# A tuned attention and MLP kernel: the second head of unit 9 is turned too, and the written-out order of the main loop is made anew

## The chip, the cores and the metric

The kernel runs on one core of a Trainium2 chip. A core has the engines TensorE (PE; its weight loads are shown as PEld), VectorE (DVE), ScalarE (ACT), GpSimd (POOL) and SyncE (SP, which here only issues DMAs). Each runs its own instructions in order and waits on semaphores for the others. The metric is the time of one execution on the device, in microseconds (us).

## The reference

One transformer block on 2048 tokens of 448 features. `xn` is the layernorm of `x`; the result is `x`, plus attention of `xn` with 16 query heads of 28 and one shared key and value head, plus an MLP (layernorm, 448 to 1792, GELU, 1792 to 448) of `xn`.

```python
q = (xn @ wq)            # 16 heads of 28
k, v = xn @ wk, xn @ wv  # one head, shared by all
scores = einsum("bhqd,bkd->bhqk", q, k) * 28 ** -0.5
p = softmax(scores, axis=-1)
attention = einsum("bhqk,bkd->bhqd", p, v) @ wo
y = layernorm(xn)
mlp = gelu(y @ w1 + b1) @ w2 + b2
out = x + attention + mlp
```

## The kernel before

The queries are cut into 4 blocks of 512, the heads into 4 groups of 4. A block and a group make a *unit*: 16 units, each with 4 heads of 512 queries against 2048 keys, the keys in 16 *key tiles* of 128. The kernel first normalises and projects, then runs the MLP, and beside the MLP it begins the attention; what is left of attention is the main loop.

There are two ways to the exponentials of a head.

- *Not turned.* A first pass computes the scores with queries on the partitions (TensorE, L668, 16 matmuls of 128x512) only to reduce each to its maximum (VectorE, L669). The maxima go into two spare rows of the query operand, and a second pass computes the scores with keys on the partitions, the maximum already taken off (TensorE, L1104, 16 matmuls); ScalarE exponentiates them from the PSUM bank into a tile `p` (L1105).
- *Turned.* One pass computes the scores with queries on the partitions (TensorE, L704, 16 matmuls). VectorE moves each to the SBUF tile `raw` with its maximum (L705); four such make a tile of 128 queries by 2048 keys. ScalarE exponentiates that in two halves (L722), four DMAs of 256 KB store it to DRAM in `td` (L725), and later it is loaded by quarters of the keys (`quarter`, L913, two DMAs of 512 KB a quarter), where VectorE turns blocks of 32x32 into `p` (L1080, one instruction for two key tiles).

Which heads are turned is in `TURNED`, pairs of unit and head: head 3 of every unit, and head 2 of units 11, 13 and 15, 19 in all. The tile `raw` has two buffers (`RAWS = 2`), so the first L705 of a tile waits for the store of the tile two before it.

From the `p` tiles of all four heads the value product goes, key tile by key tile, into one bank `po` (L1068; L1051 for the last unit, which is done in two halves): four matmuls with 32 columns of weights each, side by side in the array. A run of such products is called a *burst* here. Then the sums are divided out (`norm_jobs`) and multiplied by `wo` (`o_jobs`, L944 to L946).

The main loop goes over 128 steps of two key tiles, taken in 64 pairs, four pairs a unit. What an engine does in which order is nothing but the order in which the program issues it, and that is written out: `ORDERS` has a string for each pair, and each letter issues something. `s` is a score matmul of L1104 with its exponential, `m` a maximum (L668 and L669), `t` a step of a turned head (L704 and L705), `x` half an exponentiation of `raw` (L722, with the stores behind the second half), `T` a turn (L1080), a digit so many key tiles of the value product, as far as their `p` tiles are issued, `e` the maxima of the next unit, `n` a step of the division, `o` a step of the product with `wo`, and `|` the second step of the pair, with its loads. `BANKS` gives for each matmul that takes a PSUM bank in the loop which of the seven it takes. Beside the MLP, 192 turned steps and 390 maxima are done at a fixed pace that no table sets; the strings hold the rest, 112 `t`, 330 `m`, 720 `s` and 152 `T`. The loads of quarters are issued four steps ahead by SyncE, those of queries by GpSimd.

Of the kernel before, what the change touches and what calls it, by code (L numbers as in the profile page):

```python
# [26 lines left out]
SCALE = DH ** -0.5  # L27
PAIRS = 13
ORDERS = (
    "|sssmsmssmtmssmmmTssTtss",  # L30
    "sm|ssss3smsttsmsstTssT",
    "smmss|sm3essmtsTxmsssstsT",
    "T|x4mmsstTssmsssssm2smss",
    "mmsssmTxxsstmTmss4smn|sntsss",
    "smm2nmsmsmmsststst|Tntxsmss3enmTsmnxs",
    "ssssm3TsmnsmssttmsTsss|n",
    "ssxnmsTtsnxn22msnsmmmssssnsTs|",
    "ssstT2smsst|msmssssTs",
    "ssT|2msntmsTstsxmmnsmmx4smsnnstmsts",
    "|ssmTnmnnTsses3smssstssmsmxmm",  # L40
    "sns3sssTsmm|smnnstmmtm2snssmmsntT",
    "sssTssxnssm4mnsnmmsss|mtsT",
    "sss|2mmsmssxtmnnTsmssnxs3snsT",
    "|tmsmsssstsnssTTe21tmssssx",
    "sT|smsss1nn4Tmmxsntnssmmsmsss",
    "sssTmsnnms3Tmsmsmtnsssms|sto",
    "ntsT4xxsnsnTms|stmnstsmmssmnsnsns",
    "o2nooTmsmosmosesnsmttmTsm3msmssmsmsno|mnxos",
    "smTssTmx|4stsmnstsmsstsss",
    "Ts|mmssT3tsmmmsmsmxmtsossmsnmsnmtsmm",  # L50
    "sns|sTsssnx6nmssmsmTmtsossm",
    "smsnssmssmmstosmst|sexxTTnss",
    "ssTmsn213|snsmsmtnsnsTosmmssntns",
    "sstTsmxstxsts31mstssmTtnss|s",
    "Tsss2msnsnstsmmm|sTssssmxxn3",
    "tennmTTstnsssnmssnss4sms|sms",
    "mssmsssn|tssmTmsTsn3nttssmms",
    "ssxxmmTnsmssst1T3mntsm|ssnsss",
    "Ttsnsxtn21s|mnsssxTsmmses2msmss",
    "ssmtssmsnsstnT|s4xTmsmssms",  # L60
    "nssnstsxmTsm2mTsssssnsmtt|2s",
    "Tssnmnmtsnstsxxtmmss3on|mmosstnnsTsms",
    "smT|osso4smesnsmsmmmsssnmsnTs",
    "smnst2x2T|tsmsnsmssmosmxmosTssns",
    "msn3|sTmsmnsmossmnsnttsmsstxsTxmos",
    "sTs5mstsmsstsTmmmsso|tssttmsx",
    "sTtsoxssststnmnms2xsmmssxnsmnT|s",
    "ssmsnns5smnesTstmssm|osmssT",
    "sstsnss|Tmsnn3smtssmmnTsss",
    "ms|stnxsTm4Tsmssnssssss",  # L70
    "mm|xT2mtnmssnsm11mnnstssmsstsssTs",
    "sTm2|esnnsmssmtssmnnxmsmxsntT3msstmms",
    "so|tTstssmmTmm1n3smnssmsssnmmnsms",
    "|sTsTm5nTmnmnsmsnntssTss",
    "Ts|ssTTTss5msesnmsm",
    "ssssxssT111s|TTTs",
    "snmsssss|nTxsTT5Tntsn",
    "smmsmsssmsnttsssnnTm|mxsm3mmmnosTs",
    "Tmsmms|smsn4nmtxesnmstsnTsssmomsts",
    "nmn3|osmsmsmsmosmnmsossTmTssomsmsn",  # L80
    "4on1TnnmssmnTtsssssm|1smsmssms",
    "sTm3oTmmssnTnsmnm|omssssT",
    "msmxnsnomTssTtt4nstnmm|TssnTs",
    "ssm|sneonTnTssmsmm4TmssT",
    "mTmsmnsns5xmsTTTs|mmsss",
    "stsT4mmxnsss|snnossnmssTss",
    "sxnssmm31ssmTsssssm2Tmsnm|s",
    "ssmsmTs1enssnssss|snTs",
    "ss4ssssssTsnns|2Tss",
    "TnssssssTssT1n|11T",  # L90
    "nnTsss|ssTTsT3ss",
    "ssssssTn5n|sToTTs",
    "sTssosTs|sossoT212T",
)
BANKS = (
    "0163240513642015346203412503125064312560314526045231604521306451230465123460531246053214062153046123"
    "5024361502431652034150632451603124560312453610245631024563214056325140632510436251043652014630521463"
    "0524136052130465213406253140625310462531046253014652301426531024635102463152046312054631024563012456"
    "3102451630245610324605312460531240653214605231460521346503241560324150632145306214350621436502143650"
    "2416350241630524165340231654023165420635412063541205634120563421603542160345216034521603542160534216"  # L100
    "5034215603241653204165320145603124560314620346205134620513642105436120534610523460154236014523604152"
    "3604123560412536014256302145630214562340165234012635401623405612340561234051624305162430521463052164"
    "3052164350126431502643152064312654031265401326504150326451034265013425610234560124351602435160352416"
    "0352416035421630541263540126345012603145263015426301546230154623015642301546320154620314520631425603"
    "1426503142650312456031245601324651032465103426510342650143256013425610342615361304256013246051362540"
    "1362541063421503416025341625304162530416253041625301462503146520314650321460531240653241524063152631"
    "564023156402315640263415026341250631420563124056312405631240563124053124053124053124053124031"
)
# [10 lines left out]
def block_kernel(ctx, tc, x, wq, wk, wv, wo, w1, b1, w2, b2, out):  # L119
# [16 lines left out]
    def heads_of(u):  # L136
        return 4 - sum(v == u for v, _ in TURNED)

# [438 lines left out]
    for c in range(NCH):  # L577
        if c + 1 < NCH:
            center, turn = norm_parts(c + 1, False, bank=lambda shape: (qbank, mtile)[next(turns) % 2](shape))
        for i in range(4):  # L580
# [24 lines left out]
            if i in ((1, 3), (1, 2), (1, 3), (0, 2))[c]:  # L605
# [90 lines left out]
    def turned_scores(i):  # L696
        for t in range(CT):
# [4 lines left out]
            for n in range(4):  # L702
# [4 lines left out]
                                  op0=ALU.mult, op1=ALU.max, accum_out=m3[:, n:n + 1])  # L707
                if (t, n) == (0, 3) and 0 < i < len(TURNED) - 1:
                    load_m(*TURNED[i + 1], q3[1 - i % 2])
                if n == 3:  # L710
                    dve.tensor_reduce(m3[:, 4:5], m3[:, 0:4], axis=AX.X, op=ALU.max, negate=True)  # L711
                    exps.extend((TURNED[i], t, raw, m3, h) for h in range(2))
                yield
# [492 lines left out]
```

## Time and profile before

| | |
|---|---|
| median of 3 runs | 1054.6 us (1054.35 to 1054.74) |
| the profiled execution | 1055.69 us, span 1052.8 us |
| TensorE busy | 1043.8 us, 99% of the span |
| VectorE busy | 926.9 us, 88% |
| ScalarE busy | 720.6 us, 68% |
| GpSimd busy | 563.1 us, 53% |
| DMA | 226.17 MB, 215 GB/s on average |

An engine's busy time is the union of its instructions. Matmuls overlap: the next one starts before the last has ended, so what a matmul costs is read from the distance of starts, in the timeline. In a row of the timeline stand the start, the length, the engine, the line of the program, the operation, what it writes and reads, and in brackets how long the engine was idle before it and what ended that. In a row of the groups stand the count, the busy time, the mean length in ns, and the idle time before. The main loop begins at about 481 us and takes the rest of the span; the score matmuls of unit 8 begin at 767.3 us, of unit 12 at 907.0 and of unit 14 at 978.4.

### The profile page before, as it was taken

Reading aid. Unit: us, or ns where it says so; the run is one execution under the profiler, and the core shown is the slowest. Engines: PE = TensorE matmul, PEld = TensorE weight load, DVE = VectorE, ACT = ScalarE, POOL = GpSimd, SP = SyncE. Lnnn points to the kernel's source line nnn. Section 1 sums busy time; section 2 is a strip of 40 time slices with the busy share of each in tenths; the row PEclk is TensorE's granted clock in tenths of the full one; section 3 lists DMA queues with packets and bytes.
Section 4 is the critical chain, followed back from the end, with each engine's and each line's share of the span. In section 5 each row is a group of like instructions: output and inputs, shape, how many; then the busy total and the mean of one; then the engine's idle time right before and its main releaser. Section 6 shows DMA issues by size and latency. Waiting matters only on the chain.

```text
span 1052.8 us, 17905 instructions
## 1 busy us (share of the span) xinstructions
PE 1043.8 (99%) x5773; PEld 708.9 (67%) x5773; DVE 926.9 (88%) x1962; ACT 720.6 (68%) x1224; POOL 563.1 (53%) x704
## 2 busy tenths in 40 slices
PE   9999999999999999999999999999999999999998
PEld 8778888888888888886455545655456555456545
DVE  7889999999999899999798889788788789999775
ACT  6775555656565665556898888688878785865692
POOL 6678787677766777865145353153334233434130
PEclk9999999999999999999999999999999999999999
DMA  8865455667776767984879688687889879898791
GB/s 274 250 217 164 116 148 150 172 166 192 190 184 170 203 183 181 276 215 138 243 205 247 204 232 257 204 237 222 249 253 255 243 237 280 271 279 261 236 354 38
DMA packets 224593, 226.17 MB, mean 215 GB/s; under 512 B 18622, under 2 KB 190804, under 8 KB 224500
## 3 DMA queue, kind: packets, MB, share of 16 engines
q1 hardware_dynamic: 212084, 204.06, 67.0%
q0 software_dynamic: 11008, 20.40, 7.3%
q8 instruction: 45, 0.74, 0.3%
q10 hardware_dynamic: 1408, 0.57, 0.2%
q14 instruction: 48, 0.39, 0.1%
HBM read 129.24 MB, written 94.49 MB: 213 GB/s over the span
## 4 chain that ended last, share of the span: by engine, by line
PE 94%; DVE 3%; DMA 1%; ACT 1%; SPq 0%; issue 0%; ACTq 0%; DVEq 0%
PE po L1068 20%; PE m L1104 16%; PE m L668 16%; PE m L787 12%; PE ph L262 11%; PE m L704 7%; PE qp L262 3%; DVE mx L669 1%; PE ph L265 1%; PE ph L267 1%; PE m L944 1%; PE m L946 1%; PE m L945 1%; DMA td<-raw 1%; PE po L1051 1%; PE m L1051 1%
## 5 line engine op out<-in xcount | busy, mean ns | idle before, releaser
L669 DVE TENSOR_REDUCE mx<-m 128x1 f32<-128x512 f32 x720 | 463.6, 683 | 54.6 <-PE m L668 51.9
L1105 ACT ACTIVATE p<-m 128x512 f32<-128x512 f32 x622 | 323.6, 623 | 90.1 <-PE m L1104 88.8
L668 PE MATMUL m<-ks,qm 128*128 128x512 f32 x720 | 277.7, 401 | 1.1 <-DVE mx L669 0.6
L1104 PE MATMUL m<-xh,ks 128*128 128x512 f32 x720 | 229.8, 405 | 2.1 <-DVE raw L705 1.1
L1068 PE MATMUL po<-p,vs 128*32 128x512 f32 x1664 | 221.8, 596 | 0.0
L705 DVE TENSOR_SCALAR_CACHE_REDUCE raw<-m 128x512 f32<-128x512 f32 x304 | 202.4, 686 | 20.0 <-PE m L704 12.5
L1104 PEld LDWEIGHTS m<-xh,ks 128*128 128x128 f32 x720 | 131.6, 188 | 69.2 <-ACT p L1105 16.6
L722 ACT ACTIVATE raw<-raw,m 128x1024 f32<-128x1024 f32 x152 | 170.3, 1158 | 3.2 <-DVE m L711 3.1
L668 PEld LDWEIGHTS m<-ks,qm 128*128 128x128 f32 x720 | 134.2, 188 | 55.9 <-issue 12.6
L1080 DVE STREAM_TRANSPOSE p<-quarter 128x1024 f32<-128x1024 f32 x128 | 155.5, 1229 | 4.9 <-PE m L1104 3.1
L752 ACT ACTIVATE hx<-ph,b1t 128x512 f32<-128x512 f32 x55 | 37.9, 688 | 150.5 <-PE ph L267 99.0
L1068 PEld LDWEIGHTS po<-p,vs 128*32 128x32 f32 x1664 | 54.7, 109 | 105.0 <-issue 101.4
L704 PE MATMUL m<-ks,q 128*128 128x512 f32 x304 | 119.0, 398 | 0.0
L768 POOL TENSOR_TENSOR hl<-hx,hh 128x512 fp32r<-128x512 f32 x56 | 72.7, 1298 | 32.4 <-ACT hh L766 32.3
L787 PE MATMUL m<-w2h,hl 128*128 128x448 f32 x224 | 81.3, 367 | 0.0
L787 PE MATMUL m<-w2h,hh 128*128 128x448 f32 x224 | 81.3, 366 | 0.0
L787 PE MATMUL m<-w2l,hh 128*128 128x448 f32 x224 | 81.2, 366 | 0.0
L756 POOL TENSOR_TENSOR hz<-hz,hx 128x512 f32<-128x512 f32 x56 | 72.8, 1300 | 4.6
L761 POOL TENSOR_TENSOR hx<-hx,hz 128x512 f32<-128x512 f32 x56 | 72.6, 1297 | 4.7
L704 PEld LDWEIGHTS m<-ks,q 128*128 128x128 f32 x304 | 57.0, 188 | 20.2 <-issue 2.5
L1068 PE MATMUL po<-xh,vs 128*32 128x512 f32 x256 | 68.7, 596 | 0.0
L633 POOL DMA_DIRECT2D xh<-qd x60 | 38.0, 634 | 56.7 <-PE m L1104 34.4
(198 smaller groups left out, 1527.8 us busy)
## 6 DMA issues: line engine op xcount, KB each, us to landing
td<-raw SPq DMA_DIRECT2D x304, 256.0 KB
quarter<-td SPq DMA_DIRECT2D x146, 512.0 KB
xh<-qd POOLq DMA_DIRECT2D x48, 168.0 KB, 5.6
qd<-qe SPq DMA_DIRECT2D x24, 256.0 KB
a<-in_A_x_dram SPq DMA_DIRECT2D x24, 224.0 KB
qm<-qd SPq DMA_DIRECT2D x96, 56.0 KB
qm<-qd POOLq DMA_DIRECT2D x84, 56.0 KB, 4.9
ad<-a SPq DMA_DIRECT2D x16, 224.0 KB
```

The costliest lines, as they stand in the source:

```text
L262: pe.matmul(ps, w, v, start=(n == 0), stop=False)
L668: pe.matmul(pm, qm[:, t * P:(t + 1) * P], ks[:, n * CW:(n + 1) * CW], start=True, stop=True)
L669: dve.tensor_reduce(mx[:, CT * j + t, n:n + 1], pm, axis=AX.X, op=ALU.max)
L704: pe.matmul(sc, q3[i % 2][:, t * P:(t + 1) * P], ks[:, n * CW:(n + 1) * CW], start=True, stop=True)
L705: dve.tensor_scalar(raw[:, n].rearrange("p r (b i) -> p b r i", i=32), sc.rearrange("p (b r i) -> p b r i", r=4, i=32), SCALE, -3e38, op0= ...
L722: act.activation(raw[:, rs], raw[:, rs], AF.Exp, bias=m3[:, 4:5], scale=1.0)
L756: pool.tensor_mul(hz, hz, hx)
L787: pe.matmul(m2[k], h[:, k * P:(k + 1) * P], w[:, ft, :], start=(ft == 0 and i == 0), stop=(ft == NF - 1 and i == 2))
L1068: pe.matmul(po[32 * j:32 * j + 32, :], vs[:, kt, :], ps.pop((u, kt, j)), start=(kt == 0), stop=(kt == NT - 1))
L1080: dve.transpose(p.rearrange("p k (g j) -> p g k j", j=32), part[:, :, 32 * k:32 * k + 64].rearrange("p g (k j) -> p g k j", j=32))
L1104: pe.matmul(s, ks[:, kt * P:(kt + 1) * P], qss[u][:, j, :], start=True, stop=True)
L1105: act.activation(p, s, AF.Exp, scale=SCALE)
```

## The change

Head 2 of unit 9 is turned as well, 20 heads in all. All 64 strings and the table of banks are new. The strings hold 128 `t`, 314 `m`, 704 `s`, 160 `T`, 64 `x` (56 before) and 72 digits (95 before); the digits add up to 254 in both, and of the 256 key tiles 5 are left for after the last string (3 before). Of the tables the diff shows the pairs that the text speaks of.

```diff
 ORDERS = (
 ...
-    "smTssTmx|4stsmnstsmsstsss",
-    "Ts|mmssT3tsmmmsmsmxmtsossmsnmsnmtsmm",
+    "sxsm4xTtsnsmm|sssttstsnsxnxsTs",
+    "tsnsTs6Ttmsststsossmssso|",
 ...
-    "ssxxmmTnsmssst1T3mntsm|ssnsss",
-    "Ttsnsxtn21s|mnsssxTsmmses2msmss",
+    "T|sxsmottnsssmmsmsmxtm3T1msmmtsnnsss",
+    "Tn|smnssse2smssmsmsnTsss",
 ...
-    "sTs5mstsmsstsTmmmsso|tssttmsx",
-    "sTtsoxssststnmnms2xsmmssxnsmnT|s",
-    "ssmsnns5smnesTstmssm|osmssT",
-    "sstsnss|Tmsnn3smtssmmnTsss",
+    "ssT5sTTmtsmTnsnmss|s",
+    "o|TTs4snsnmmsmnmTsTssmnsmx",
+    "T|Tsnsss4essmstTsmTmo",
+    "ssntsTsmx4TnnmTsT|sss",
 ...
-TURNED = tuple((u, j) for u in range(16) for j in ((3, 2) if u in (11, 13, 15) else (3,)))
+TURNED = tuple((u, j) for u in range(16) for j in ((3, 2) if u in (9, 11, 13, 15) else (3,)))
```

On TensorE, in unit 10 before, two bursts of two key tiles stand seven matmuls apart (L1068; a key tile is four products, whose `p` tiles lie in buffers named `p` and `xh`):

```order
L668 MATMUL m_9680<-ks,qm_162 128x512
L1068 MATMUL po<-p,vs 32x512 x8
L668 MATMUL m_9702<-ks,qm_162 128x512
L704 MATMUL m_9707<-ks,q_165 128x512
L668 MATMUL m_9712<-ks,qm_162 128x512
L1104 MATMUL m_9715<-xh,ks 128x512
L1104 MATMUL m_9718<-xh,ks 128x512
L1104 MATMUL m_9722<-xh,ks 128x512
L668 MATMUL m_9725<-ks,qm_163 128x512
L1068 MATMUL po<-p,vs 32x512 x5
L1068 MATMUL po<-xh,vs 32x512 x2
L1068 MATMUL po<-p,vs 32x512
```

About the same number of scores into the loop, the new order has:

```order
L1104 MATMUL m_9813<-xh,ks 128x512
L668 MATMUL m_9817<-ks,qm_164 128x512
L668 MATMUL m_9820<-ks,qm_164 128x512
L1068 MATMUL po<-p,vs 32x512 x18
L1068 MATMUL po<-xh,vs 32x512
L1068 MATMUL po<-p,vs 32x512
L668 MATMUL m_9848<-ks,qm_164 128x512
L668 MATMUL m_9851<-ks,qm_164 128x512
L1104 MATMUL m_9854<-xh,ks 128x512
```

The two bursts of two are one of five. Over the loop 76 bursts have become 69.

On VectorE, the tile of turned scores that is begun soonest after the exponentiation of the tile two before it. Tiles are counted through the loop from 0. Before, it is tile 16, in the second of the pairs `ssxxmm...` and `Ttsnsx...` above; the last row is its first eviction, and the rows begin behind the second `x` of tile 14 and one reduction:

```order
L669 TENSOR_REDUCE mx<-m_8388 128x1
L1080 STREAM_TRANSPOSE p<-quarter 128x16x2x32
L669 TENSOR_REDUCE mx<-m_8399 128x1
L705 TENSOR_SCALAR raw,m_8347<-m_8411 128x4x4x32
L1080 STREAM_TRANSPOSE p<-quarter 128x16x2x32
L669 TENSOR_REDUCE mx<-m_8433 128x1
L705 TENSOR_SCALAR raw,m_8347<-m_8438 128x4x4x32
L711 TENSOR_REDUCE m_8347<-m_8347 128x1
L669 TENSOR_REDUCE mx<-m_8445 128x1
L912 MEMSET quarter 1x1 x2
L1080 STREAM_TRANSPOSE p<-quarter 128x16x2x32
L705 TENSOR_SCALAR raw,m_8473<-m_8474 128x4x4x32
```

In the new order it is tile 11, which begins with `tsnsTs6...`; the second `x` of tile 9 is the one behind the 4 of the pair ahead of it, and is issued just ahead of the first row:

```order
L1080 STREAM_TRANSPOSE p<-quarter 128x16x2x32
L705 TENSOR_SCALAR raw,m_7440<-m_7441 128x4x4x32
L669 TENSOR_REDUCE mx<-m_7450 128x1
L669 TENSOR_REDUCE mx<-m_7453 128x1
L912 MEMSET quarter 1x1
L705 TENSOR_SCALAR raw,m_7440<-m_7467 128x4x4x32
L705 TENSOR_SCALAR raw,m_7440<-m_7470 128x4x4x32
L705 TENSOR_SCALAR raw,m_7440<-m_7476 128x4x4x32
L711 TENSOR_REDUCE m_7440<-m_7440 128x1
L1080 STREAM_TRANSPOSE xh<-quarter 128x16x2x32
L912 MEMSET quarter 1x1
L705 TENSOR_SCALAR raw,m_7505<-m_7506 128x4x4x32
```

All four evictions of tile 10 now stand between, and fewer reductions; the first eviction comes behind nine instructions instead of eleven, the memsets left out.

More of the change, by code (lines that the diff above doesn't have):

```diff
@@ L29 @@
 ORDERS = (
[L30 to L48, printed above, removed]
-    "smTssTmx|4stsmnstsmsstsss",
-    "Ts|mmssT3tsmmmsmsmxmtsossmsnmsnmtsmm",
[L51 to L56, printed above, removed]
@@ L70 @@
[L70 to L83, printed above, removed]
@@ L84 @@
[L84 to L93, printed above, removed]
+    "ssmsmssmmmssmTmssTs|ss",
+    "tss|4TtstssmsstmsmstsssT",
+    "Tsxsm|4estssmsmssmtsmsmTss",
+    "ssxssTTms5smsmssmmmsms|s",
+    "sstssxmTtxm3mmnmsnstTssns|ssms",
+    "Tss3|stnnmssmmssmtssTsxss",
@@ new lines @@
+    "smT|nssxs6Teststmsmsstssnsnn",
+    "TsnssT|mss3tsmsnstsmmsssmmx",
+    "sTxsmsnns|s4Tmsmtsssmsnss",
+    "nssnT|tsT3sstsstsmmsntsssx",
+    "Tst|smsx4nnnTesmsmnsmtssssxss",
+    "ssm4Tsmmssmss|nnstsmTsss",
+    "|snTnsnm2ssmmsmssmsssmsmttxT3msm",
+    "sstnTs|nssmmsmxT3smsmsnnntsssmm",
+    "tmmsxsns|s3TstmesmtsTnssxsnss",
+    "n|Tts5nxsmsssmTstmsnmsss1nss",
+    "|nmstmtssTmstTsssms4omsmmomsssn",
+    "sss|onnmTsmmxn3sTmemnsotssstosss",
+    "mmxnT|tss3smsnmnsmmssmssmsTsnmms",
+    "sxsm4xTtsnsmm|sssttstsnsxnxsTs",
@@ new lines @@
+    "tsnsTs6Ttmsststsossmssso|",
+    "nTs2s|mssmmntsssstttssssm3To",
+    "3xnxTsmss|nmsnmTmsnemsssxomsssmsm",
+    "|sTssnsnsTsmontsnmmnmtxssts4smsm",
+    "|ssmntTsnssTxstmxstm4mtsnsnstsms",
+    "sns|xTs5nxesmnmstsssnstmsssT",
+    "T|snsnomstsmssstsTttss2sns",
+    "|ssmmssmmtxnnm5xTmstssmssnTsss",
+    "T|sxsmottnsssmmsmsmxtm3T1msmmtsnnsss",
+    "Tn|smnssse2smssmsmsnTsss",
+    "sstnx|mx4nTtsmstsssnmmmsssTsns",
+    "TssT3|stssnmmssssxsnss",
+    "m|mx3Tstsstsnmmmmmssnm4oooooTmtssnonsmsosmsm",
@@ new lines @@
+    "sTn|tmmxT4xsmsmsmssmntsmststnnsss",
+    "|smtsmTsm3stemsssmmmsTnmsmsmnss",
+    "xTmmn4|ssmssnmmsnnsmtTsssntxsss",
+    "ssT5sTTmtsmTnsnmss|s",
+    "o|TTs4snsnmmsmnmTsTssmnsmx",
+    "T|Tsnsss4essmstTsmTmo",
+    "ssntsTsmx4TnnmTsT|sss",
+    "sssnmnnmt4tnsstsxmsm|mTnmxossssmnsT",
+    "ns|Toesssnmmststnsnmmntxxtmmm4mmssmmsmsmsT",
+    "|ssTssmnnssmmT5mmsstsnstsms",
+    "T|mssmtmomsstTsm2sntsmmssstmsxs",
+    "T|mnmmT5msmnTTsstnsssss",
+    "Tn4sTmssnm|TnsmsnTsss",
+    "TTsxs4men|sssnsssTT",
@@ new lines @@
+    "sTsnTssTx51snTm|msmss",
+    "mmssmsxnmssTssmnn2mnmsmsTstssn|",
+    "ss1ssm|tsmnssmttTttsxoxmt4esoosnnmssmmT",
+    "ssonssmtT|sn3smmnssmssmnnmTss",
+    "xossxTsmomTt5mos|msnmssmnmsmssss",
+    "|sTmTsnTs3msntostsnToss",
+    "smsmmnsTTtsnsTsn6|Tss",
+    "TstmsnmtnTostsxmsTe7Txnmssm|ts",
+    "Tnnssmnosmsmn|TmxxnttTsTosss",
+    "s|TTst6tsmmmsnnssmxmsss2sss",
+    "TmtststTssts3xnnxmmsssmsmnnmsxsm|s",
+    "ssTs3ensnsTssns|ssss",
+    "sT3s|nssssTssssn3sns",
+    "Ts|snssssT2nnTssT",
+    "TsTsTss2ssnn|Tss",
@@ L94 @@
+    "ssss2TsTsooso4TsoT|",
+    "sssTssssT|s3TT",
 )
 BANKS = (
[L96 to L105, printed above, removed]
@@ L106 @@
-    "1362541063421503416025341625304162530416253041625301462503146520314650321460531240653241524063152631"
-    "564023156402315640263415026341250631420563124056312405631240563124053124053124053124053124031"
+    "0163240516324053126543126043512604352106342510634251063425016324051632450163245013465201345620135640"
+    "2135640213546023150426314502631450236451203645102364150236145023641502346510324653102465301425603145"
+    "2063145206345120163452061345260314526031456230145632104562314056234105623401526354021635410256431025"
@@ new lines @@
+    "6431026540635142063510462504635120641325063412506342105634251064235106425316042530416523041562031465"
+    "2103465210346521304652130465132064532104653210463045621340526314052631450264352106435210463521046352"
+    "1064532106453126045132604513624015362453016243501264350126435012645031642501346250143560214365021436"
+    "5021436510423651402635401263540126345012506342156043201456320146503421650342165304261354601235406213"
+    "5402615324103416520431650234160523416052431605431260541302564325160425361402610523460512346051234061"
@@ L108 @@
+    "5342016532401635204165302416530246153206543120643512046351024631052460351420653210465231046532106532"
+    "4106532406513245061324506132405163025461302564130526134052164350216043521604351260435612045361240356"
+    "1203456102435604132560143520641352601453601245631024651302465132046513204635104635210462315046231506"
+    "42351604325610345216304521630452163045216304521630452130452130452130415230415"
 )
-TURNED = tuple((u, j) for u in range(16) for j in ((3, 2) if u in (11, 13, 15) else (3,)))
+TURNED = tuple((u, j) for u in range(16) for j in ((3, 2) if u in (9, 11, 13, 15) else (3,)))
```

7 lines of the change are left out of this document (removed).

## The prediction, made before the change was run

> **What bounds the kernel now.** I read the page's busy times first, then the windows of the main loop, then the waits of TensorE, and only then single instructions.
>
> ```profile
> span 1052.8 us, 17905 instructions
> PE 1043.8 (99%) x5773; PEld 708.9 (67%) x5773; DVE 926.9 (88%) x1962; ACT 720.6 (68%) x1224; POOL 563.1 (53%) x704
> 480.00:1020.00 540.00, 537.75 (x3252) 288.04 (x3254) 458.86 (x939) 424.35 (x791) 202.30 (x323) 1.00 0.82 244
> 767.30:978.40 211.10, 211.10 (x1287) 115.52 (x1286) 188.61 (x381) 154.05 (x287) 81.84 (x129) 1.00 0.86 260
> 907.00:978.40 71.40, 71.40 (x433) 39.86 (x433) 67.45 (x133) 45.51 (x87) 29.44 (x45) 1.00 0.86 261
> PE m L1104 <- DVE raw L705: 1.1, 1, 1.1
> PE m L668 <- DVE mx L669: 0.6, 1, 0.6
> DVE mx L669 <- PE m L668: 51.9, 51, 4.2
> ```
>
> The window rows give the length, the busy time of PE, PEld, DVE, ACT and POOL, the granted clock, the DMA share and GB/s. From 480 to 1020 us, which is the main loop, TensorE is busy 537.75 of 540 us at full clock. VectorE is the runner-up, 188.61 of 211.1 us in units 8 to 13 and 67.45 of 71.4 us in the last two of them. TensorE waits for VectorE a microsecond at a time, VectorE for TensorE 51.9 us in all. So the time of the loop is the sum of what TensorE issues. But a busy TensorE is not one at its peak, so the price of a matmul has to come from the distance between starts:
>
> ```profile
> 700.51 0.41 PE L1104 MATMUL m<-xh,ks 128*128 128x512 f32 x1
> 700.85 1.92 PE L1068 MATMUL po<-p,vs 128*32 128x512 f32 x16
> 703.47 0.59 PE L1068 MATMUL po<-xh,vs 128*32 128x512 f32 x1
> 703.90 0.59 PE L1068 MATMUL po<-xh,vs 128*32 128x512 f32 x1
> 704.42 0.50 PE L668 MATMUL m<-ks,qm 128*128 128x512 f32 x1
> 704.76 0.40 PE L1104 MATMUL m<-xh,ks 128*128 128x512 f32 x1
> 705.00 0.40 PE L704 MATMUL m<-ks,q 128*128 128x512 f32 x1
> 705.24 0.63 PE L1104 MATMUL m<-xh,ks 128*128 128x512 f32 x2
> 705.71 0.39 PE L668 MATMUL m<-ks,qm 128*128 128x512 f32 x1
> 705.93 0.39 PE L704 MATMUL m<-ks,q 128*128 128x512 f32 x1
> 706.16 1.58 PE L1104 MATMUL m<-xh,ks 128*128 128x512 f32 x6
> 700.92 3.57 PE po L1068 x32
> 707.75 1.85 PE po L1068 x16
> ```
>
> The first number of a row is the start. From 704.76 to 706.16 six matmuls start, 0.235 us each, though one lasts 0.40. The last two rows are from the chain that ended last: a burst of four key tiles holds 3.57 us, one of two 1.85, so a key tile of the value product costs 0.86.
>
> **The change part by part.**
>
> *Matmuls.* A head that is turned has no pass for maxima (16 matmuls of L668) and no scores at L1104 (16), but 16 at L704. On TensorE 16 go: 16 x 0.235 = **-3.8 us**. They all stand in the main loop, since the stage ahead of it still takes 192 turned and 390 maximum steps. The two ends of this term are 0.235, the plain distance, and 0.40, the busy time (6.4 us); starts are what the next matmul waits for, so I take the first. On the page "TensorE: Matmul & The Clock Gate" (section Back-to-back issue gap) the Trainium skill puts a stream of weight load and matmul at 512 columns at about 131 ns each. By that the term would be an estimated 2.1 us; the rows above do not agree with it.
>
> *Bursts.* A burst costs more than its key tiles. The matmul ahead of it takes 0.34 to the first product (700.51 to 700.85) where 0.235 is usual; its last pass takes 0.52 (703.90 to 704.42) where 0.43 is usual (703.47 to 703.90); and the first matmul behind takes 0.34 again (704.42 to 704.76). That is 0.105 + 0.09 + 0.105 = 0.30 us. The strings have 95 digits before and 72 now, but digits with no matmul between them make one burst. Counted in TensorE's own order, there are 76 bursts before and 69 now, for the same 256 key tiles: 7 x 0.30 = **-2.1 us**. Both ends: 23 bursts would be -6.9, and none 0.
>
> *VectorE.* It loses 16 reductions and gains 16 evictions and 8 transposes:
>
> ```profile
> 503.72 1.24 DVE L1080 STREAM_TRANSPOSE xh<-xl 128x1024 f32<-128x1024 f32 x1
> 504.89 1.24 DVE L1080 STREAM_TRANSPOSE xh<-quarter 128x1024 f32<-128x1024 f32 x1
> 512.54 1.89 DVE L669 TENSOR_REDUCE mx<-m 128x1 f32<-128x512 f32 x3
> 519.17 0.69 DVE L705 TENSOR_SCALAR_CACHE_REDUCE raw<-m 128x512 f32<-128x512 f32 x1 [3.59 <-DMA td<-raw]
> 519.78 0.08 DVE L705 DVE_READ_ACCUMULATOR raw<-m 128x1 f32 x1
> ```
>
> By starts a transpose is 1.17 us (503.72 to 504.89), a reduction 0.60 (1.89 less 0.69, by two), an eviction 0.61 plus up to 0.06 for its accumulator. So VectorE gets 16 x 0.07 + 8 x 1.19 = 10.6 us more, with the tiny memset of the loads. It lies beside TensorE's work as long as there is room. In units 8 to 13 the new strings hold 138 reductions, 46 evictions and 72 transposes, which make 82.8 + 30.8 + 85.7 and some 7 us of small ones: 206 us. By the prices above TensorE issues 205 us there. That looks like a tie, but units 12 and 13 of before held 56 reductions, 9 evictions and 24 transposes, some 71 us beside 69 of TensorE, and the last window row above shows TensorE busy in all of them. So I take 0.5 us, between 0 and 3.
>
> *ScalarE.* It loses 16 exponentials and gains 8 of twice the width:
>
> ```profile
> L1105 ACT ACTIVATE p<-m 128x512 f32<-128x512 f32 x622 | 323.6, 623 | 90.1 <-PE m L1104 88.8
> L722 ACT ACTIVATE raw<-raw,m 128x1024 f32<-128x1024 f32 x152 | 170.3, 1158 | 3.2 <-DVE m L711 3.1
> ```
>
> That is 8 x 1.16 - 16 x 0.62, about nothing, and it mostly waits for TensorE. No price.
>
> *DMA.* 16 stores of 256 KB and 8 loads of 512 KB are new, 8.4 MB.
>
> ```profile
> q1 hardware_dynamic: 212084, 204.06, 67.0%
> ```
>
> 204 MB took 67% of the span, 3.5 us for a megabyte over all engines, so 29 us in a loop of some 500: a DMA share of 0.82 becomes about 0.88. The loads are issued four pairs of steps ahead, and VectorE nowhere waits for one. The stores are another matter. There are two buffers for raw scores, so the first eviction of a tile of 128 queries waits until the tile two before it has been exponentiated and stored. Queued behind that eviction on VectorE are the reductions and evictions that free TensorE's banks:
>
> ```profile
> 507.86 3.33 SPq L725 DMA_DIRECT2D td<-raw  x4
> 519.92 0.50 PE L1104 MATMUL m<-xh,ks 128*128 128x512 f32 x1 [1.10 <-DVE raw L705]
> 522.25 1.09 PE L1104 MATMUL m<-xh,ks 128*128 128x512 f32 x3 [0.51 <-DVE mx L669]
> 734.02 2.22 ACT L722 ACTIVATE raw<-raw,m 128x1024 f32<-128x1024 f32 x2
> 736.26 3.63 SPq L725 DMA_DIRECT2D td<-raw  x4
> 742.92 0.69 DVE L705 TENSOR_SCALAR_CACHE_REDUCE raw<-m 128x512 f32<-128x512 f32 x1 [0.69 <-DMA td<-raw]
> DVE raw L705 <- DMA td<-raw: 4.9, 4, 3.6
> ```
>
> From issue to the eviction it takes 6.7 us at the good place (736.26 to 742.92) and 11.3 at the bad one (507.86 to 519.17). At the good place the second exponential begins at about 735.1, so 7.8 us lie between it and the eviction, 0.69 of them idle. Between the letter of that exponential and the letter of the eviction the strings have five reductions, two evictions and three transposes, 7.9 us of VectorE's work. The other tiles have more, and of the four waits in the last row only the one at the bad place was long. In the new strings five tiles have less: tile 11 of the loop has two transposes, four evictions and two reductions, 6.3 us (TensorE only 16 matmuls, 3.8), and tiles 8, 17, 30 and 14 have 6.5, 6.7, 7.3 and 7.5, by the longer of the two engines. Against a need of about 8.2 they are 1.9, 1.7, 1.5, 0.9 and 0.7 short, 6.7 us on VectorE. Of the idle 3.59 us at the bad place TensorE lost some 2 (1.10, 0.51 and smaller steps), of the 0.69 none. So I take **+2.0 us** for these, between 0 and 6.7. At the bad place itself the tile's way is about 1.8 us shorter than before on TensorE, but 1.2 longer on VectorE; I take 0, from -2 (the stall goes) to +1.8.
>
> *The end.* The last eight key tiles run after the last score, as before, with eight score matmuls now put just ahead of them and four transposes to be done meanwhile, 4.8 us beside 1.9 + 6 x 0.86 = 7.1 until the last of them is read. No price, up to +1.
>
> **Sum.** -3.8 - 2.1 + 0.5 + 2.0 = -3.4 us. The profiled execution took 1055.69 us, 2.9 of it outside its span of 1052.8, and would take 1052.3; the median of the runs is 1.1 below it, and the same difference off that median, 1054.6, gives **1051.2 us**.
>
> **The rivals.**
>
> *The waits eat the gain.* VectorE is at 206 against 205 us in units 8 to 13, and the five short tiles fall partly into units without slack. If TensorE pays all 6.7 us of the short tiles, or half of them and the 3 of the tie, the 5.9 us won are gone: about 1055. For it speaks that 0.69 us idle could be seen already; against it that units 12 and 13 ran at this load without loss, and that four of the five tiles stand in units 3 to 7, where by the same count VectorE has 4 us and more of room in a unit.
>
> *Stores come back late.* This one ends slower. A store that takes 11.3 us instead of 6.7 adds 4.6 us of idle VectorE at a short tile, of which TensorE pays some 60%, 2.8 us. Two of them on top of the sum give +2.2, and from there on it decides; three give +5.0, about 1059.6. For it speaks the higher DMA share; against it that of the four waits before only one was long. The Trainium skill, "DMA: Bandwidth & Descriptors", section Latency and other measured facts, gives HBM access as 0.2 us on average and 2 us at high load, so by that rule the stores would slow down as the share rises. The bad place, with wo's loads in the same queue, is the only one here that looks like it.
>
> *Only the matmuls count.* If the burst's surcharge is a stall that moves elsewhere, -2.1 drops out of the sum: 1053.3, within 0.2%.
>
> *No new waits at all.* -5.9, and -7.9 if the bad place heals: 1046.7 to 1048.7.
>
> **How the numbers follow.** About 0.2%, 2.1 us, is what a measurement can tell from no change. The sum with small waits (-2.1 to -5.2) gets 0.47, no new waits 0.15, the eaten gain 0.15, only the matmuls 0.08, late stores 0.15. Faster by over 0.2% are the first two, 0.62; within are the eaten gain and only the matmuls, less a little that crosses the line, 0.20; slower are the late stores and that little, 0.18. The likeliest case spans 1049.4 to 1052.5. For 8 in 10 the range leaves out the best of the no-wait case and the worse half of the late stores: 1047.8 to 1057.
>
> **What would show it.** TensorE's busy time in the loop falls about as the span does; L668 and L1104 have 704 each, L704 320; the distances within and around a burst stay 0.235, 0.34, 0.52 and 0.34. The wait of the raw eviction for its store grows from 4.9 us to some 10 over about nine times, with waits of TensorE for L705 or L669 behind the long ones. Wrong I would be if TensorE showed gaps of several microseconds behind these evictions, or if it waited for transposes in units 9 to 13.

## The result, and the profile after

| | before | after |
|---|---|---|
| median | 1054.5 us (1054.35 to 1054.74) | 1047.4 us (1046.87 to 1048.25) |
| the profiled execution | 1055.69 us, span 1052.8 | 1048.25 us, span 1046.4 |
| ratio | | 0.9933, 95% interval 0.9916 to 0.995 |

The change gains 7.1 us, 0.67%. The forecast was 1051.2 us with a range from 1047.8 on: the time lies 0.4 us below that range, and the gain is twice the forecast one. By the interval of the ratio the gain is 5.3 to 8.9 us, so the edge of the range can't be told from the measurement, but the forecast gain of 3.4 can.

The first lines of the page of after, and the queue that SyncE issues to:

```profile
span 1046.4 us, 17964 instructions
PE 1037.4 (99%) x5757; PEld 704.9 (67%) x5757; DVE 935.1 (89%) x1998; ACT 722.8 (69%) x1216; POOL 562.0 (54%) x704
...
q1 hardware_dynamic: 221684, 212.45, 69.8%
```

The windows of the loop (480 to 1020 us) and of its units 8 to 13, in the columns that the prediction explained:

```profile
480.00:1020.00 540.00, 538.70 (x3295) 289.68 (x3295) 471.44 (x980) 431.47 (x793) 204.45 (x324) 1.00 0.88 261
759.50:971.40 211.90, 211.15 (x1281) 115.59 (x1278) 200.08 (x409) 149.38 (x274) 80.47 (x130) 1.00 0.93 278
```

TensorE is busy 6.4 us less, and the span is 6.4 shorter. It has 16 matmuls less (5757). VectorE is busy 8 us more, and in units 8 to 13 it is now busy 200 of 212 us (188.61 of 211.1 before). The DMA share of the loop is 0.88, the number that was forecast.

The waits of VectorE that answer to those shown of before:

```profile
DVE mx L669 <- PE m L668: 29.7, 38, 2.4
DVE raw L705 <- PE m L704: 18.3, 34, 1.8
DVE p L1080 <- DMA quarter<-td: 7.2, 4, 4.1
```

VectorE waits 22 us less for the maxima's matmuls and 6 us more for the turned scores' (12.5 before), so it has less room. A row of the raw eviction waiting for its store, which was 4.9 us before and should have grown to 10, isn't there any more. In its place turns (L1080) wait for their quarters, at 562, 815, 949 and 1009 us; before, none did in the loop by the view. A fifth turn waits 4.7 us at 1002; the view puts it down to a matmul here, and in another run of the same kernel to its quarter.

The distances of starts, behind a burst at 693 us of after:

```profile
693.35 0.60 PE L1068 MATMUL po<-p,vs 128*32 128x512 f32 x3
693.37 0.59 PE L1068 MATMUL po<-xh,vs 128*32 128x512 f32 x1
693.89 0.50 PE L668 MATMUL m<-ks,qm 128*128 128x512 f32 x1
694.23 0.40 PE L704 MATMUL m<-ks,q 128*128 128x512 f32 x1
694.47 0.85 PE L1104 MATMUL m<-xh,ks 128*128 128x512 f32 x3
695.16 0.39 PE L704 MATMUL m<-ks,q 128*128 128x512 f32 x1
```

They are those of before: some 0.52 for the last pass, 0.34 for the first matmul behind, 0.23 for the others. The medians over all bursts of the loop agree: 0.33 from the matmul ahead to the burst, 0.52 and 0.34, the same before and after. So the loop can be split into what TensorE issues and what it waits. The first is its instructions at 0.231 us for a matmul of 512 columns, 0.201 for one of 448, 0.108 for one product of a burst, and 0.30 for a burst; the second is the rest of the time between the first scores of one unit and the next. (The last two units hold 7 us of it in both: the end, which issues little.)

| | issued | waits in units 0, 1 | 2 to 7 | 8 to 13 | 14, 15 | loop |
|---|---|---|---|---|---|---|
| before | 550.1 | 5.5 | 5.2 | 3.7 | 7.4 | 572.0 |
| after | 544.3 | 2.7 | 4.6 | 6.8 | 7.1 | 565.6 |
| difference | -5.8 | -2.8 | -0.6 | +3.1 | -0.3 | -6.4 |

What TensorE issues, so the trace's counts times its distances, went down by 5.8 us; the prediction had 5.9. The error lies in the waits, for which it had added 2.5 us; in these two executions they fell by 0.6.

### The profile page after: what moved, and what is told of

The parts are those of the page before. It is cut to its first block, busy times and chain, and to the rows that moved or that the text cites. A ratio compares the mean times of both kernels' runs of the same rounds, so it can differ in the third digit from the quotient of the medians.

```text
span 1046.4 us, 17964 instructions
## 1 busy us (share of the span) xinstructions
PE 1037.4 (99%) x5757; PEld 704.9 (67%) x5757; DVE 935.1 (89%) x1998; ACT 722.8 (69%) x1216; POOL 562.0 (54%) x704
## 4 chain that ended last, share of the span: by engine, by line
PE 91%; DVE 4%; DMA 3%; issue 1%; ACT 1%; ACTq 0%; DVEq 0%
PE po L1068 19%; PE m L1104 15%; PE m L668 15%; PE m L787 12%; PE ph L262 11%; PE m L704 7%; PE qp L262 3%; DMA quarter<-td 2%; DVE mx L669 2%; PE ph L265 1%; PE ph L267 1%; PE m L944 1%; PE m L946 1%; PE m L945 1%; DVE p L1080 1%
## 5 line engine op out<-in xcount | busy, mean ns | idle before, releaser
L669 DVE TENSOR_REDUCE mx<-m 128x1 f32<-128x512 f32 x704 | 451.8, 682 | 32.3 <-PE m L668 29.7
L1105 ACT ACTIVATE p<-m 128x512 f32<-128x512 f32 x612 | 318.1, 633 | 79.8 <-PE m L1104 78.2
L668 PE MATMUL m<-ks,qm 128*128 128x512 f32 x704 | 268.6, 399 | 1.6 <-DVE mx L669 0.6
L705 DVE TENSOR_SCALAR_CACHE_REDUCE raw<-m 128x512 f32<-128x512 f32 x320 | 212.3, 684 | 22.0 <-PE m L704 18.3
L1104 PE MATMUL m<-xh,ks 128*128 128x512 f32 x704 | 223.6, 406 | 0.0
L1068 PE MATMUL po<-p,vs 128*32 128x512 f32 x1664 | 221.0, 595 | 0.4 <-DVE p L1080 0.4
L722 ACT ACTIVATE raw<-raw,m 128x1024 f32<-128x1024 f32 x160 | 180.1, 1165 | 4.4 <-DVE m L711 4.2
L1104 PEld LDWEIGHTS m<-xh,ks 128*128 128x128 f32 x704 | 127.6, 188 | 68.4 <-issue 15.9
L1080 DVE STREAM_TRANSPOSE p<-quarter 128x1024 f32<-128x1024 f32 x133 | 161.1, 1228 | 7.6 <-DMA quarter<-td 7.2
L1068 PEld LDWEIGHTS po<-p,vs 128*32 128x32 f32 x1664 | 55.6, 109 | 109.2 <-issue 103.1
L704 PE MATMUL m<-ks,q 128*128 128x512 f32 x320 | 125.5, 399 | 0.0
L704 PEld LDWEIGHTS m<-ks,q 128*128 128x128 f32 x320 | 59.8, 188 | 22.2 <-issue 5.0
L1068 PE MATMUL po<-xh,vs 128*32 128x512 f32 x256 | 68.2, 596 | 0.0
```

The lines of the kernel that those rows point to most:

```text
L668: pe.matmul(pm, qm[:, t * P:(t + 1) * P], ks[:, n * CW:(n + 1) * CW], start=True, stop=True)
L669: dve.tensor_reduce(mx[:, CT * j + t, n:n + 1], pm, axis=AX.X, op=ALU.max)
L704: pe.matmul(sc, q3[i % 2][:, t * P:(t + 1) * P], ks[:, n * CW:(n + 1) * CW], start=True, stop=True)
L705: dve.tensor_scalar(raw[:, n].rearrange("p r (b i) -> p b r i", i=32), sc.rearrange("p (b r i) -> p b r i", r=4, i=32), SCALE, -3e38, op0= ...
L722: act.activation(raw[:, rs], raw[:, rs], AF.Exp, bias=m3[:, 4:5], scale=1.0)
L1068: pe.matmul(po[32 * j:32 * j + 32, :], vs[:, kt, :], ps.pop((u, kt, j)), start=(kt == 0), stop=(kt == NT - 1))
```

## The experiments

**The price of a burst.** The changed kernel with 29 bursts cut in two, four matmuls between the halves (98 bursts, nothing else changed); two of the strings:

```diff
-    "o|TTs4snsnmmsmnmTsTssmnsmx",
-    "T|Tsnsss4essmstTsmTmo",
+    "o|TTs2snsnmm2smnmTsTssmnsmx",
+    "T|Tsnsss2essms2tTsmTmo",
```

> The changed kernel with two key tiles of most bursts of four and more put four matmuls later: 98 bursts instead of 69, the same products. Theory (a burst costs 0.30 us beside its key tiles): 29 x 0.30 = 8.7 us slower, 1056.1. Rival (the surcharge is a stall that would come anyway, and shorter bursts feed VectorE and ScalarE more evenly): no slower, or up to 2 us.

Measured: 1059.2 us, ratio to before 1.0037 (1.0023 to 1.005), 10.6 above the changed kernel on the same chip. By the count above, the loop issues 8.7 us more, 29 x 0.30, and the medians around its 98 bursts are again 0.33, 0.52 and 0.34. The loop of its profile is 10.1 us longer; the rest is waits, 3.5 more in unit 14 and less elsewhere. The surcharge of a burst is a price and doesn't move elsewhere, so "only the matmuls count" falls.

**The price of a matmul.** One score matmul in eleven is issued twice, 64 in all; the second repeats the first.

```diff
-        pe.matmul(s, ks[:, kt * P:(kt + 1) * P], qss[u][:, j, :], start=True, stop=True)
+        for _ in range(2 if kt % 4 == j == 0 else 1):
+            pe.matmul(s, ks[:, kt * P:(kt + 1) * P], qss[u][:, j, :], start=True, stop=True)
```

> The changed kernel with 64 of its score matmuls issued twice into the same bank (head 0 of every fourth key tile), so 64 matmuls of TensorE more and no work for any other engine. Theory (the loop costs what TensorE issues, 0.235 us a matmul): 15.0 us slower than the changed kernel, 1062.4. By the busy time of a matmul, 0.40 us: 25.6 slower, 1073. By the 0.131 us that the skill's page gives: 8.4 slower, 1055.8. If TensorE had room: less than 5.

Measured: 1057.7 us, ratio 1.0032 (1.0019 to 1.0045), some 10.4 above the changed kernel by the ratios (1.0032 and 0.9933 of the same kernel): 0.16 us each. The loop issues 14.8 us more (64 x 0.231), and the waits fall from 21.3 to 17.4. Neither figure of the prediction is the net price, and the 15 us expected did not come. A matmul costs its distance, but it also gives the other engines that time, and a quarter to a third of it comes back. If that holds the other way round, 16 matmuls fewer were worth less than 3.8 us, where all engines are nearly full. By the same share some 1 us of the new waits in units 8 to 13 would be that; this is an estimate and wasn't measured there.

**Fewer bursts still.** In five places a short digit is added to the next one, which makes 65 bursts of the 69. The last of them:

```diff
-    "sT3s|nssssTssssn3sns",
+    "sTs|nssssTssssn6sns",
```

> The changed kernel with five digits moved into the burst behind them, the first four or five near the end of the loop: 65 bursts instead of 69. Theory: 4 x 0.30 = 1.2 us faster, 1046.2. Rival (longer runs of scores without a burst starve TensorE of banks, because ScalarE and VectorE free them more slowly than it takes them): the gain goes, or up to 2 us slower.

Measured: 1053.0 us, ratio 0.9984 (0.9971 to 0.9997), 4.4 slower than the changed kernel beside it, though it issues 1.2 us less. Unit 14, where this string and another of the five stand, lost 4.1 us, and unit 5, where the first stands, 1.8. The window of the long run of scores there, with the columns of the windows:

```profile
1000.00:1004.50 4.50, 4.50 (x11) 1.71 (x10) 0.00 (x0) 4.50 (x11) 1.78 (x4) 1.00 0.95 285
```

and its rows of the timeline:

```profile
999.40 4.53 ACT L1105 ACTIVATE p<-m 128x512 f32<-128x512 f32 x9
1000.55 0.19 PEld L1104 LDWEIGHTS m<-xh,ks 128*128 128x128 f32 x1 [0.30 <-ACT p L1105]
1001.04 0.19 PEld L1104 LDWEIGHTS m<-xh,ks 128*128 128x128 f32 x1 [0.30 <-ACT p L1105]
```

TensorE counts as busy all the time, but ten matmuls in a row start 0.49 us apart, each behind an exponential that frees its bank (nine take 4.53 us). ScalarE is full and VectorE does nothing. In this place a burst is not only a cost: while it runs, ScalarE can catch up.

**The order without the head.** The new strings for 19 heads: the first 16 `t` are `m`, eight `x` are dropped, each second `T` of unit 9 is two `s`, the banks are given anew.

```diff
-    "ssT5sTTmtsmTnsnmss|s",
-    "o|TTs4snsnmmsmnmTsTssmnsmx",
+    "ssT5sssTmtsmssnsnmss|s",
+    "o|Tsss4snsnmmsmnmTsssssmnsmx",
```

> The new order with the second head of unit 9 not turned: the first 16 turned steps of the strings become maxima, their 8 halves of exponentiation go, and in unit 9 each second turn becomes two scores, with banks for them. It has 69 bursts as the new order has, and the same start but for the missing turned tiles. Theory (the gain is what TensorE issues, 3.8 us for the 16 matmuls and 2.1 for the bursts, and some 2.5 more from a stall at the start that is gone): 3.8 us slower than the changed kernel, so 1051.2, 0.3% under the kernel before. Rival (the written-out order alone made the gain, the turned head gave nothing because VectorE pays for it): about 1047.4. Rival (the head gave all, the order nothing): about 1054.5.

Measured: 1055.6 us, ratio 1.0023 (1.0011 to 1.0035), by the ratios 9.5 above the changed kernel and beyond all three expectations. The loop of its profile is 8.6 us longer than that of after. It issues 3.7 us more, as 16 matmuls should, and the rest is waits, 4.6 of them in unit 9, where the scores were put in. TensorE waits for ScalarE there, the longest in the waits of the window from 797 to 836 us:

```profile
PE m L1104 <- ACT p L1105: 1.7, 3, 1.1
PE m L668 <- ACT p L1105: 0.5, 1, 0.5
```

The rest are steps of some tenths behind these. The likely reason is that two scores in the place of a turn give ScalarE two exponentials close together, in strings that were not made for it. So this run shows that the new order is no gain by itself where its letters are replaced, but not what the head and the order are worth apart. A written-out order and its letters can't be separated by replacing letters.

**The start.** Two kernels take the stall near 518 us out of the kernel before. The first has the new order's first eight strings and the old ones from there on, the second only an `x` 14 letters sooner:

```diff
-    "smmss|sm3essmtsTxmsssstsT",
-    "T|x4mmsstTssmsssssm2smss",
+    "smmss|sm3essmtsTxxmsssstsT",
+    "T|4mmsstTssmsssssm2smss",
```

> The kernel before with the first eight strings (units 0 and 1) of the new order and their banks; two maxima, two steps of the division and one half exponentiation are added at the end of the eighth so that the rest fits. 74 bursts instead of 76, 19 heads. Theory (some 2.5 us of the gain is the stall near 518 us, which the new strings do not have): 2.5 + 2 x 0.3 = 3.1 us faster than before, 1051.4. Rival (the stall is a chance of DMA traffic and comes at another place, or the start does not matter): 0.6 us faster, 1053.9.

> The kernel before with one letter moved: the second half of the exponentiation of the loop's first tile is issued right behind its first half, some 14 letters earlier, so that its store is issued ahead of the loads of the next step and of wo. Theory (the stall near 518 us comes from this store being late for the eviction two tiles on): the 3.6 us that VectorE waits there go, and 2 us of TensorE with them: 1052.4. Rival (the stall has another cause, such as too many matmuls for the banks): the same time as before, within 0.5 us.

Measured: 1054.2 us, ratio 1.0007 (0.9998 to 1.0017), for the first, 1053.2 us, ratio 0.9995 (0.9985 to 1.0004), for the second. Neither gained what was expected. In the first the waits of units 0 and 1 fell to 3.1 us, but unit 2 and 3, where old strings meet new ones, lost 2.1. In the second the waits of units 0 and 1 fell to 3.0 and nothing came back elsewhere: its span is 2.0 us shorter than that of the profile of before, and still the median is only 0.3 below. That fits if the profiled execution of before had a longer stall than most. So the kernel before was profiled again:

> The kernel before once more, for a second look at the loop's start. Theory (the stall near 518 us, 2 to 3 us of TensorE in units 0 and 1, is in every execution, and its absence is part of what the change won): units 0 and 1 again hold 5 to 6 us above what TensorE issues there, and the eviction again waits 3 to 4 us for its store. Rival (the stall comes and goes, as the small gain of the kernel with the earlier exponentiation suggests): units 0 and 1 hold 3 to 4 us, the wait is under 1.5 us, and the difference of the two kernels in a run without it is some 5 us instead of 7. Time 1053 to 1055 by both.

Measured: 1054.3 us, ratio to the other runs of the same kernel 0.9993 (0.9983 to 1.0002); its profiled execution took 1053.0 us, span 1050.9. The eviction that waited 3.59 us now is

```profile
517.42 0.69 DVE L705 TENSOR_SCALAR_CACHE_REDUCE raw<-m 128x512 f32<-128x512 f32 x1 [1.72 <-DMA td<-raw]
```

Half as long, and it stands for all of the 1.9 us between the two spans: the waits of units 0 and 1 are 3.7 us instead of 5.5, the other stretches of the table are the same to a tenth. So both theories were half right. The stall is there in both profiles of before, 0.7 to 2.6 us of TensorE above the version without it, and a single profile says little about its size.

**The stores.** If the short tiles have the margin that the prediction denied, it should be small. The second exponentiations ahead of the five were put 8 matmuls later, and in another kernel sooner (8 for two of them, 1 or 2 for the rest, where the first half of the tile leaves no more room). Tile 11's:

```diff
-    "sxsm4xTtsnsmm|sssttstsnsxnxsTs",
+    "sxsm4Ttsnsmm|sssxttstsnsxnxsTs",
```

> The changed kernel with the second half of the exponentiation issued eight matmuls later for the tiles whose store the tiles 8, 11, 14, 17 and 30 of the loop wait for, which leaves 2 to 4.5 us between that letter and the eviction instead of 6.3 to 7.5. It measures what the prediction priced at 2.0 us for the order as it is. Theory (the new order keeps just enough there, some 7.3 us from the exponential's start to the eviction): VectorE now waits some 2 to 3 us at each of the five, 10 to 14 in all, and TensorE pays over half of what exceeds a microsecond: 4 to 8 us slower, 1051 to 1055. Rival (there is much more room than counted, since VectorE runs behind TensorE and catches up later): under 1.5 us slower.

> The second exponentiations ahead of the five short tiles are issued sooner, by 8 matmuls for tiles 8 and 14, by 1 or 2 for tiles 11, 17 and 30. Theory (in the changed kernel no raw eviction waits for its store, so the margin that the prediction priced at 2.0 us costs nothing): the same time within 0.7 us. Rival (the stores cost something that the waits do not name): 1 to 2 us less.

Measured: 1071.3 us, ratio 1.0152 (1.0126 to 1.0178), later; 1049.3, ratio 0.9944 (0.9932 to 0.9957), sooner. The second is 0.9 above the changed kernel beside it (1048.4), a little more than the 0.7 expected, and surely no gain, so there is nothing to win; what it lost in its profile is 0.9 in unit 3, where the exponentiation now stands ahead of scores. The first lost 22.7 us, where 4 to 8 were expected: beside the profile of after, its waits are 24 us longer in units 3 to 7 and 14, in which the five tiles lie, and 1.4 shorter in unit 13. Its waits of VectorE and of TensorE:

```profile
DVE raw L705 <- DMA td<-raw: 19.3, 5, 6.4
DVE raw L705 <- ACT p L1105: 5.1, 1, 5.1
PE m L1104 <- DVE raw L705: 9.1, 4, 3.7
PE m L668 <- DVE raw L705: 2.5, 2, 1.5
```

Eight matmuls are at least 1.9 us, and all five tiles wait. The first row holds 0.5 us from ahead of the loop and the waits of tiles 11, 14, 17 and 30 (6.4, 4.4, 4.6 and 3.3 us). The second is that of tile 8: the view puts it down to ScalarE, but the last packet of the store ended 0.5 us ahead of the eviction, as it did 0.5 to 1.0 us ahead of the other four. That is 23.9 us of VectorE, 4.8 a tile. The order as made leaves its stores little room, but enough. TensorE stands still for only 11.6 us behind these evictions and loses 24. Part of the difference is the clock, whose mean over this execution is 0.993 instead of 1.000, an estimated 7 to 8 us. The longest of TensorE's waits in the timeline,

```profile
743.80 0.69 DVE L705 TENSOR_SCALAR_CACHE_REDUCE raw<-m 128x512 f32<-128x512 f32 x1 [4.62 <-DMA td<-raw]
744.55 0.80 PE L1104 MATMUL m<-xh,ks 128*128 128x512 f32 x1 [3.73 <-DVE raw L705]
```

and the windows around it:

```profile
742.00:745.00 3.00, 0.45 (x1) 0.45 (x2) 1.20 (x3) 0.00 (x0) 0.00 (x0) 0.73 0.85 166
745.00:748.00 3.00, 3.00 (x10) 1.59 (x13) 3.00 (x7) 2.23 (x3) 0.00 (x0) 0.50 0.77 291
```

Behind a pause of 3.73 us the granted clock is 0.50 for some microseconds.

**The late load.** The changed kernel was run twice more, and once with unit 9's loads of quarters spread. At 806 us six of them are issued at one place, because the `|` of one pair stands at its end and that of the next at its start:

```diff
-    "ssT5sTTmtsmTnsnmss|s",
-    "o|TTs4snsnmmsmnmTsTssmnsmx",
+    "ssT5s|TTmtsmTnsnmsss",
+    "oTTs4snsnm|msmnmTsTssmnsmx",
```

> The changed kernel as it is, beside the three that follow, as their base. It should take 1047.4 us within 0.7.

> The changed kernel a third time, beside the version with the earlier loads. Theory (units 0 and 1 are free of the stall, the late load of unit 9 comes in some executions only): units 0 and 1 hold 2.5 to 3.5 us of waits, units 8 to 13 between 6 and 11 by whether a turn in unit 9 waits 0.5 or over 2 us for its load; 1047 to 1049. Rival (the order itself puts no bound on the start): a store wait of over 2 us shows up in units 0 to 2.

> In unit 9 the six loads of quarters that are issued at one place (806 us) are spread: the second step of the unit's first pair begins 13 letters sooner, that of the second pair 9 letters later. Theory (the wait of the turn at 815 to 817 us is that of a load issued too late in a full queue): the first of these loads is issued near 802 us, the wait of L1080 for its quarter in unit 9 is gone, the unit loses no clock, and the time is 0.5 to 1.5 us below the changed kernel's on the same chip. Rival (the DMA engines are full there, and a load issued sooner only shares with the others): the wait stays between 0.5 and 5 us, or moves to the next turns, and the time is the same within 0.5 us.

Measured: 1048.6 us, ratio 0.9936 (0.9914 to 0.9959); 1048.4, ratio 0.9935 (0.9922 to 0.9949); with the loads spread 1048.7, ratio 0.9937 (0.9925 to 0.995). The first one's profiled execution was its slowest, 1051.8 us; unit 9 waits 4.5 us in it, 1.0 in after and 0.9 in the third. A turn came late there, behind it the operands of a product with `wo`, and with them TensorE:

```profile
816.98 1.25 DVE L1080 STREAM_TRANSPOSE p<-quarter 128x1024 f32<-128x1024 f32 x1 [2.08 <-DMA quarter<-td]
820.16 0.45 PE L944 MATMUL m<-xl,oth 128*128 128x448 f32 x1 [2.32 <-DVE mn L654]
822.10 0.57 PE L944 MATMUL m<-xl,oth 128*128 128x448 f32 x1
822.48 0.57 PE L945 MATMUL m<-xl,oth 128*128 128x448 f32 x1
```

and the window behind it, with the granted clock third from the end:

```profile
820.00:824.00 4.00, 3.84 (x12) 3.44 (x13) 4.00 (x7) 0.00 (x0) 2.52 (x5) 0.58 1.03 387
```

The wait of 2.08 us on VectorE costs 2.32 on TensorE, and then the matmuls of 448 columns go at 0.38 us instead of 0.20 while the clock is down. (Another 1.4 us came in unit 15.) Spreading the loads didn't help. SyncE was still issuing stores until 801.4 us, and the first two of the six were issued at 803.62 and 805.39 instead of 806.26 and 806.68. The turn waited as it did:

```profile
798.12 3.27 SPq L725 DMA_DIRECT2D td<-raw  x4
801.49 16.80 SPq L913 DMA_DIRECT2D quarter<-td  x10
816.67 2.42 DVE L1080 STREAM_TRANSPOSE p<-quarter 128x1024 f32<-128x1024 f32 x2 [1.73 <-DMA quarter<-td]
```

Unit 9 has 2.2 us of waits in it. So the rival's outcome came. In after the window from 805 to 820 us reads

```profile
805.00:820.00 15.00, 14.63 (x95) 7.98 (x88) 14.30 (x29) 9.66 (x19) 3.71 (x8) 1.00 1.02 313
```

a DMA share of 1.02: the loads share full engines. With the queue's packets counted off in order, the load that was issued 2.6 us sooner began its first at 810.3 us (809.7 in after) and ended at about 813.5 in both. What a larger shift would do isn't shown.

## Why the prediction missed

*Matmuls, -3.8, and bursts, -2.1: right.* The counts and the distances of the trace give 5.8 us less, and the split kernel bears out the price of a burst. That the price is nearer the distance of starts than the busy time held too. But as a net price the distance is an upper figure: the doubled kernel paid 0.16 us a matmul and not 0.235.

*The short raw tiles, +2.0: this is the step that failed.* Charged were 6.7 us of VectorE over five tiles, and 2.0 of TensorE. In three executions of the changed kernel only tile 11 waited for its store, 0.4, 0.2 and 0.9 us; no wait of TensorE stands behind it, and in units 2 to 7, which hold four of the five tiles, the waits fell by 0.6. The prediction needed 8.2 us between the letter `x` and the eviction, and gave the shortest tile, 11, 6.3 by VectorE's work. (At the good place the whole way was 7.8 with its wait; nothing in the lines gives 8.2.) In the trace of after it is:

```profile
641.37 1.22 ACT L722 ACTIVATE raw<-raw,m 128x1024 f32<-128x1024 f32 x1
642.62 2.99 SPq L725 DMA_DIRECT2D td<-raw  x4
646.50 0.50 PE L704 MATMUL m<-ks,q 128*128 128x512 f32 x1
648.73 0.69 DVE L705 TENSOR_SCALAR_CACHE_REDUCE raw<-m 128x512 f32<-128x512 f32 x1 [0.39 <-PE po L1068]
```

From issue to eviction it is 6.1 us (6.7 at the good place of before). The view puts the idle 0.39 us down to a matmul of `po`, which this eviction doesn't read; its own matmul had ended at 647.0. The last packet of the store ended 0.5 us ahead of it, as at the good place of before and in the third run, where the same wait (0.86 us) is put down to the store. So it most likely is the store here too. The way is 7.4 us from the start of the exponentiation, not 6.3: VectorE took the eviction 2.2 us after its matmul had started, and had waited 0.75 us for a matmul on the way. The instructions between two letters give a lower bound of the time between them, and on an engine that runs behind or waits it was more. The need was set too high by taking one wait of 0.69 us, in one execution, as if each store took that long: in the second profile of before the same eviction waited 0.14. And the prediction had read itself that TensorE lost nothing by it. In the other four short tiles the store had landed 1.6 to 4.4 us ahead.

*The start, 0, between -2 and +1.8: the mechanism was seen, the size was not.* The stall went. Between the first profiles of the two kernels the waits of units 0 and 1 fell by 2.8 us, between before's second and after's third by 1.0. It was a wait on one store whose length differs from execution to execution. The prediction took the long one it saw as the rule, and then let it stay. So this is the second term that failed, put at 0: with the charge for the short tiles left out the sum would have been 1049.2 us, still 1.8 above the measured time.

*VectorE, +0.5, between 0 and 3: too low.* The waits in units 8 to 13 grew by 3.1 us (2.5 in the third run). VectorE's 200 of 212 us shows how near the tie is; 0.7 us each came in units 8 and 10, in steps of a tenth that no row of waits names, the rest in units 9 and 13, behind late quarters (unit 12 in the third run). That TensorE would wait for transposes in units 9 to 13 was named among the signs of a wrong forecast, and it came, if only by 0.4 us at 951 us in the profile of after. This error worked against the other two: with 0.5 us of such waits the time would have been some 2 us lower still.

*ScalarE and the end, 0: right* for this kernel; the merged version shows how near ScalarE is, locally.

*DMA: share right, consequence wrong.* It was the loads that came late, in a stretch at 1.02, not the stores. "VectorE nowhere waits for one" held for before only. (The loads are issued four steps ahead, as stands with the kernel, and not four pairs.)

*The rivals.* "No new waits at all" (1046.7 to 1048.7) is the case that came, in its sum if not in its parts: new waits of 2.5 to 3.1 us in units 8 to 13 are paid by those that went at the start and in units 2 to 7. It had 0.15, and the range had left out its better half. "The waits eat the gain" and "stores come back late" did not come.

*What stays open.* The same account between before's second profile, 570.0 us for the loop, and after's third, 565.3, gives -4.7 for the loop: -5.8 issued, -1.0 at the start, -0.6, +2.5 and +0.1 further on. The medians of the three comparisons say -6.2 to -7.1. Of that, 0.4 to 0.7 lies outside the span (a median of 2.1 to 2.5 us in the runs of before, 1.8 in those of after), which no trace explains. The rest is that the median execution of before is over 1 us slower than its second profile; the stall at the start can be only part of it, since the kernel before with the earlier `x`, which has no such stall, has a median just 0.3 us lower, at most 1.6 by its interval. What the head and the new order are worth apart is open too.

## What to carry to other kernels

Count what the bounding engine issues, at the distance of its starts: that term came out to a tenth, and the waits around it, which fell in some units and rose in others, nearly cancelled; that they did was luck. Where all engines are nearly full, take it as an upper figure: a matmul that was added alone cost 0.16 us of its 0.23. A margin of a wait that is read from one execution and from counted instructions should not be charged at all unless the trace of before shows that the bounding engine lost time by it; keep it for the range. Look next at stretches, not sums: runs of scores that fill ScalarE, and loads that bunch where the DMA share is over 1, are where the next microseconds went.

## What was not expected of the hardware

A pause of TensorE costs more than itself. Behind 2.32 us of it the granted clock was 0.58 on the mean of a window of 4 us, behind 3.73 us 0.50 for three. In the kernel with the late exponentiations two more places tell that a shorter pause can do it:

```profile
608.00:612.00 4.00, 2.51 (x16) 1.43 (x9) 1.44 (x4) 2.06 (x4) 0.15 (x1) 1.00 0.89 269
612.00:616.00 4.00, 4.00 (x22) 2.39 (x21) 3.88 (x9) 3.57 (x7) 1.50 (x2) 1.00 1.05 338
701.00:706.00 5.00, 3.12 (x12) 1.17 (x8) 3.17 (x8) 2.29 (x5) 1.94 (x3) 0.99 0.95 256
706.00:710.00 4.00, 4.00 (x17) 1.88 (x21) 3.08 (x9) 3.10 (x6) 0.00 (x0) 0.59 1.11 321
```

The second window stands behind 1.5 us idle out of four, and the clock stays full; the fourth stands behind 1.9 us idle out of five, and the clock is 0.59. The longest single pauses there were 1.49 and 1.57 us, and in the kernel with the loads spread 1.54 us at 819 left the clock at 1.00. What decides between them isn't shown. On the page "TensorE: Matmul & The Clock Gate", section "HAM oscillation — how this bites in real kernels", the Trainium skill gives the rule that no gap should be over some 3.4 us. Here less was enough, and the measurement decides. With it one late load, 2.08 us of VectorE, cost unit 9 3.5 us.

A matmul that is added costs less (0.16 us) than the 0.231 us between starts: the waits of the loop fell by 3.9 us beside 14.8 issued.
